# Pairing value loads by free cells, and the last output projection ahead of the last values, in a streaming attention decode kernel

## The chip, the cores and the metric

One core of a Trainium2 chip runs the whole kernel. The metric is the device time of one execution in microseconds (us), as the median of several. All executions quoted here are of the fast state; executions of one and the same kernel still spread by 0.4 to 1.5% (the changed kernel: 1161.5 to 1171.7 us in ten, 0.9%). Verdicts come from ratios: the mean time of one kernel's fast runs over that of the other's fast runs of the same rounds, with a 95% interval. Such a ratio is not quite the ratio of the medians that stand beside it.

## The reference, cut to what matters

Two layers, run twice over one batch of 8 with one query position each. D = 512, 32 query heads on 8 key/value heads, a cache of 8192 positions, head size 128, everything in bf16.

```python
x = A_x
x = x + attention(layernorm(x), A_k_cache, A_v_cache, A_wq, A_wo)
x = x + silu(layernorm(x) @ B_w1) @ B_w2
x = x + attention(layernorm(x), A_k_cache, A_v_cache, A_wq, A_wo)   # same caches, same weights
x = x + silu(layernorm(x) @ B_w1) @ B_w2
```

Keys of a batch are loaded once and used for both layers while they are on chip; values are loaded twice. That makes 465 MB from HBM for a few vectors of result.

## The kernel before: the parts that matter here

A small planner in the kernel lays out all work before the program is built: it simulates loads and engine work with assumed durations, gives each load a place in SBUF and decides the order of instructions on every engine. On the chip, loads are issued by one queue in that order, each as soon as the readers of its place are done. Values go through a ring of 7 cells of 4 KB per partition. One value head (2 MiB) is four quarters; a quarter is 128 rows of 4 KB, and two quarters side by side are one load of 8 KB rows. Before, the code says at each call whether a head comes as two halves or four quarters:

```python
RATE = {1: 2.57, 2: 2.51, 4: 2.48}     # assumed us per MiB for 1, 2, 4 cells
...
def load_v(b, g, q, cells):
    src = A_v_cache[b, g].rearrange("(p y) d -> p (y d)", p=128)
    return load_cells(f"v{b}.{g}.{q}", cells, [(lambda buf: buf, src[:, GR * q:GR * (q + cells)])])
...
# the calls
a_values(made[v], cells=1 if b >= 0 and i >= len(vs) - 3 else 2)
values(made[v], cells=1 if i < 2 else 2)
```

A load of two cells waits in the plan, and so in the queue's order, until two neighbouring cells are free.

The end of the program: wo (the weights of the output projection) for the last layer came in rows of 1 KB, behind three of the last six value heads:

```python
wo_v = A_wo.rearrange("(h p) d -> p h d", p=128)
...
for g, k in ((2, 0), (3, 1), (4, 2)):
    values(made[g], at=k)
load_wo_all()
for g, k in ((5, 5), (6, 6), (7, 7)):
    values(made[g], at=k)
# then: projection and feed-forward of batches 0..6, then those of batch 7
```

## Time and profile before

| | before |
|---|---|
| median of 3 runs | 1177.71 us (1177.63 to 1178.75) |
| span of the profiled run | 1177.4 us |
| DMA queue, share of 16 engines' span | 98.1% |
| busiest compute engine | PE, 61% |
| last value landing to the end | 15.3 us |

How to read it: the DMA share says that almost every us of the span is paid for by bytes in flight, so a us can be won in three ways only: bytes that move faster, engines that stop being idle, or a shorter piece after the last byte. The lines themselves stand in the prediction. In them PE is the matrix engine (PEld its weight loads), DVE, ACT and POOL are the engines for elementwise work, and an SPq line is the queue that issues loads.

### The profile page before, as it was taken

To read this page: it belongs to the slowest core of one execution; us is meant where nothing else is said; L and a number is where in the kernel's file an instruction comes from. 1 tells how busy PE (TensorE), PEld (TensorE's weight loads), DVE (VectorE), ACT (ScalarE), POOL (GpSimd) and SP (SyncE) were. 2 spreads that over 40 slices of the span, in tenths; PEclk is the share of its full clock that TensorE was granted. 3 is DMA by queue.
4 is the path that set the end of the run, shared out by engine and by line. 5 is a ranking of instruction groups with operands and counts; after the bars stand their busy time and mean duration, and the time that the engine had idled before them with its cause. 6 is when DMAs were issued, how large, how long until landed. Compare 5 with 4: busy or idle time off the path is not lost.

```text
span 1177.4 us, 32188 instructions
## 1 busy us (share of the span) xinstructions
PE 718.1 (61%) x13836; PEld 374.4 (32%) x13836; DVE 599.4 (51%) x1718; ACT 138.5 (12%) x477; POOL 117.5 (10%) x296
## 2 busy tenths in 40 slices
PE   2544556675565755666566665567556675565957
PEld 1222333242332423223232333224233242322535
DVE  5652356625565255733657245662556525573331
ACT  0010011111111111111111111111111111011110
POOL 1000011101111000100111001110111100010110
PEclk9655676757777577766667566775777666575775
DMA  9999799999999999999999999999999999999994
GB/s 365 421 420 338 307 421 420 413 403 400 415 407 411 387 413 417 414 404 386 422 423 413 401 404 410 410 404 395 409 416 403 408 394 408 419 415 394 400 394 167
DMA packets 85838, 467.15 MB, mean 397 GB/s; under 512 B 8880, under 2 KB 14784, under 8 KB 62144
## 3 DMA queue, kind: packets, MB, share of 16 engines
q1 hardware_dynamic: 85696, 465.10, 98.1%
q8 instruction: 109, 1.79, 0.6%
q14 instruction: 33, 0.27, 0.1%
HBM read 465.05 MB, written 0.01 MB: 395 GB/s over the span
## 4 chain that ended last, share of the span: by engine, by line
DMA 79%; PE 16%; issue 2%; DVE 1%; SPq 1%; ACT 0%; POOL 0%; POOLq 0%; DVEq 0%; ACTq 0%
DMA ring<-in_A_v_cache_dram 73%; PE ot L871 8%; PE sc L748 4%; DMA kts<-in_A_wo_dram 2%; DMA w<-in_B_w_dram 1%; DMA ring<-in_A_wq_dram 1%; PE misc L642 1%; PE yt L944 1%; DMA kts<-in_A_v_cache_dram 1%; PE sc L723 1%; SPq L340 0%; PE misc L510 0%; PE ex L893 0%; PE ex L915 0%; PE misc L492 0%
## 5 line engine op out<-in xcount | busy, mean ns | idle before, releaser
L871 PE MATMUL ot<-ring,p 128*8 128x256 bf16 x3904 | 243.5, 360 | 197.5 <-DMA ring<-in_A_v_cache_dram 195.8
L694 DVE STREAM_TRANSPOSE kts<-kts 128x1024 uint32<-128x1024 uint32 x256 | 309.1, 1226 | 36.8 <-DMA kts<-in_A_k_cache_dram 36.3
L748 PE MATMUL sc<-kts,bd 128*32 128x256 bf16 x4096 | 291.7, 406 | 34.4 <-DVE kts L694 24.8
L871 PEld LDWEIGHTS ot<-ring,p 128*8 128x8 bf16 x3904 | 73.5, 90 | 281.6 <-DMA ring<-in_A_v_cache_dram 261.2
L885 DVE TENSOR_TENSOR part<-ot,p 128x256 bf16<-128x256 f32 x128 | 54.2, 424 | 194.9 <-PE sc L748 95.1
L748 PEld LDWEIGHTS sc<-kts,bd 128*32 128x32 bf16 x4096 | 114.4, 117 | 103.2 <-DVE kts L694 34.1
L765 POOL PARTITION_ALL_REDUCE small<-small x128 | 47.8, 373 | 651.2 <-DVE small L761 536.6
L774 ACT ACTIVATE expd<-sc,small 128x256 bf16<-128x256 f32 x128 | 60.7, 475 | 416.1 <-DVE small L769 400.5
L881 ACT ACTIVATE p<-ot 128x256 bf16<-128x256 f32 x128 | 49.1, 384 | 469.5 <-PE ot L871 468.5
L780 PE MATMUL sc<-expd,ident 128*32 128x256 bf16 x512 | 42.8, 324 | 86.9 <-ACT expd L774 86.3
L794 POOL PARTITION_ALL_REDUCE small<-small x128 | 56.3, 440 | 197.7 <-DVE small L790 197.7
L760 DVE TENSOR_REDUCE small<-sc 128x1 f32<-128x256 f32 x128 | 53.3, 417 | 18.4 <-PE sc L748 18.4
L787 DVE STREAM_TRANSPOSE p<-sc 128x256 bf16<-128x256 bf16 x128 | 55.9, 437 | 9.3 <-PE sc L780 5.8
L731 DVE TENSOR_TENSOR bd<-sc,mask 128x64 bf16<-128x64 f32 x128 | 28.0, 219 | 56.2 <-PE sc L748 50.4
L780 PEld LDWEIGHTS sc<-expd,ident 128*32 128x32 bf16 x512 | 15.0, 107 | 126.2 <-ACT expd L774 126.0
L790 DVE TENSOR_SCALAR small<-hm,small 128x4 f32<-128x4 f32 x128 | 27.1, 212 | 37.1 <-ACT expd L774 37.1
L893 PE MATMUL ex<-diag,p 128*128 128x4 bf16 x256 | 25.5, 169 | 25.6 <-DVE part L885 23.2
L893 PEld LDWEIGHTS ex<-diag,p 128*128 128x128 bf16 x256 | 16.8, 103 | 73.5 <-ACT p L881 45.9
L944 PEld LDWEIGHTS yt<-z,ring 128*128 128x128 bf16 x1024 | 31.5, 101 | 26.1 <-issue 26.1
L944 PE MATMUL yt<-z,ring 128*128 128x4 bf16 x1024 | 36.4, 166 | 4.3 <-DVE z L922 4.0
L922 DVE TENSOR_TENSOR z<-ex,rc 128x16 bf16<-128x16 f32 x64 | 11.2, 174 | 54.6 <-PE ex L915 54.4
L723 PE MATMUL sc<-qab,sel 128*128 128x4 bf16 x256 | 16.3, 170 | 32.6 <-DVE rc L798 21.7
(84 smaller groups left out, 489.1 us busy)
## 6 DMA issues: line engine op xcount, KB each, us to landing
ring<-in_A_v_cache_dram SPq DMA_DIRECT2D x260, 512.0 KB, 8.2
kts<-in_A_k_cache_dram SPq DMA_DIRECT2D x64, 2048.0 KB, 11.2
ring<-in_A_v_cache_dram SPq DMA_DIRECT2D x114, 1024.0 KB, 11.7
ring<-in_A_wo_dram SPq DMA_DIRECT2D x64, 512.0 KB, 11.6
ring<-in_A_wq_dram SPq DMA_DIRECT2D x36, 512.0 KB, 9.6
kts<-in_A_v_cache_dram SPq DMA_DIRECT2D x5, 2048.0 KB, 16.7
kts<-in_A_wo_dram SPq DMA_DIRECT2D x2, 2048.0 KB, 27.0
w<-in_B_w_dram SPq DMA_DIRECT2D x2, 1792.0 KB, 14.7
```

The lines of the kernel that those rows point to most:

```text
L694: op(dve, lambda: dve.transpose(v, v), reads=[], writes=[res("kt", g)], add=(q > 0))
L748: steps.append(lambda t=t, y=y, w=w: pe.matmul(sc[32 * t:32 * t + 32, 0:256], w, kv[:, 2 * t + y, q], start=(q == 0 and y == 0), stop=(q = ...
L760: op(dve, lambda: dve.tensor_reduce(mxr[si], sv, AX.X, ALU.max), reads=[res(*scr)], writes=[res("mxr", si)])
L765: op(pool, lambda: pool.partition_all_reduce(mxa[si], mxp[si], 128, bass.bass_isa.ReduceOp.max), reads=[res("mxp", si)], writes=[res("mxa" ...
L774: op(act, lambda: act.activation(pe_out[:, :], sv, ACT.Exp, bias=bias[si], scale=SM_SCALE, accum_out=rsum[si]), reads=[res(*scr), res("bia ...
L780: steps = [lambda P=P: pe.matmul(sc[32 * P:32 * P + 32, 256:512], src[:, P], pe_out[:, :], start=True, stop=True) for P in range(4)]
L787: op(dve, lambda: dve.transpose(pt[:, :], src), reads=[res(*scr)], writes=[res("p", sm)])
L794: op(pool, lambda: pool.partition_all_reduce(ssa[si], ssm[si], 128, bass.bass_isa.ReduceOp.add), reads=[res("mxp", si)], writes=[res("mxa" ...
L871: steps.append(lambda t=t, c=c, k=k: pe.matmul(ot[32 * t:32 * t + 2 * R, 0:2 * DH], pt[:, k:k + 2 * R], vt[:, c, t], start=(P == 0 and c = ...
L881: op(act, lambda: act.activation(pt[:, :], ot[:, 0:2 * DH], ACT.Copy), reads=[res("ot", o)], writes=[res("p", sm)])
L885: op(dve, lambda: dve.tensor_tensor(part[:, :], ot[:, 0:2 * DH], pt[:, :], ALU.subtract), reads=[res("ot", o), res("p", sm)], writes=[res( ...
L944: steps.append(lambda j=j, dt=dt: pe.matmul(YT[:, dt * R:(dt + 1) * R], w[:, j, dt * 128:(dt + 1) * 128], zt[:, R * j:R * j + R], start=(g ...
```

## The change

Its intent: let the planner pair two quarters into a half wherever two cells side by side happen to be free, wait for a pair only while more than 2 us of transfers are still queued, and otherwise take a single cell; give wo of the last layer 4 KB rows; load it ahead of the last six value heads, so that the projection and feed-forward of batches 0 to 6 need not run at the very end. The core of the diff (cuts marked; the comments behind `#` in this and the later diffs are mostly added here, as labels):

```diff
-    RATE = {1: 2.57, 2: 2.51, 4: 2.48}
+    RATE = {1: 2.66, 2: 2.52, 4: 2.52}
+    ENOUGH = 2.0
...
+                        at = self.place(idle, n.cells)
+                        mate = n.mate if ... loads[li + 1] is n.mate and n.mate.left == 0 else None
+                        if mate:
+                            two = self.place(idle, 2)
+                            if two is not None:
+                                at = two
+                            else:
+                                mate = None
+                                if at is not None and wire - now > self.ENOUGH + 0.01:
+                                    at = None          # wait: enough is queued
...
-        values(h, cells=1)         # and the other calls
+        values(h)
...
-    wo_v = A_wo.rearrange("(h p) d -> p h d", p=128)
+    wo_v = A_wo.rearrange("(g p j) d -> p g (j d)", g=G, j=R)
...
-    for g, k in ((2, 0), (3, 1), (4, 2)):
-        values(made[g], at=k)
     load_wo_all()
...
+    for g, h in enumerate(made):
+        if g > 1:
+            values(h, at=g)
+        ...
+        w = out_proj_a(h, w, h["u"])      # per head, behind that head's values
```

With 4 KB rows four neighbouring rows of wo lie in one partition, so the attention output must be spread by a selection matrix and masked before the product (as layer 0 did already). The selection matrices become stride-4 views of four identities.

More of the change, by code (lines that the diff above doesn't have):

```diff
@@ L115 @@
 class Node:
-    __slots__ = ("eng", "dur", "emit", "prio", "deps", "outs", "left", "ready", "end", "take", "give", "name", "cells")
+    __slots__ = ("eng", "dur", "emit", "prio", "deps", "outs", "left", "ready", "end", "take", "give", "name", "cells",
+                 "mate", "span")
     def __init__(self, name, eng, dur, emit, prio, deps):
@@ L133, in __init__ @@
         self.cells = 0
+        self.mate = None
+        self.span = 1
 class Plan:
-    RATE = {1: 2.57, 2: 2.51, 4: 2.48}
+    RATE = {1: 2.66, 2: 2.52, 4: 2.52}
+    ENOUGH = 2.0
     LAND = 5.0
@@ L188, in run @@
         wire = 0.0
+        alarm = 0.0
         idle = set(cells)
@@ L200, in run @@
                     n = loads[li]
-                    at = self.place(idle, n.cells) if n.take else None
+                    at = mate = None
+                    if n.left == 0 and n.take:
+                        at = self.place(idle, n.cells)
+                        mate = n.mate if li + 1 < len(loads) and loads[li + 1] is n.mate and n.mate.left == 0 else None
+                        if mate:
[6 more added lines that the diff above has]
+                                    at = None
+                                    if wire - self.ENOUGH > alarm:
+                                        alarm = wire - self.ENOUGH
+                                        heapq.heappush(events, (alarm, seq, "alarm", n))
+                                        seq += 1
                     if n.left == 0 and (at is not None or not n.take):
@@ L205, in run @@
                             idle -= set(range(at, at + n.cells))
+                        dur = n.dur
+                        if mate:
+                            n.span = 2
+                            mate.give = at + 1
+                            mate.span = 0
+                            idle.discard(at + 1)
+                            dur = self.RATE[2]
                         order.append((now, seq, n))
                         seq += 1
-                        wire = max(wire, now + 0.1) + n.dur
+                        wire = max(wire, now + 0.1) + dur
                         heapq.heappush(events, (wire + self.LAND, seq, "done", n))
@@ L211, in run @@
                         li += 1
+                        if mate:
+                            order.append((now, seq, mate))
+                            seq += 1
+                            heapq.heappush(events, (wire + self.LAND, seq, "done", mate))
+                            seq += 1
+                            li += 1
                         moved = True
@@ L277, in _build @@
     w2_sb = sb([128, FT, D], BF16, "w2")
-    ident = sb([128, 128], BF16, "ident")
+    ident4 = sb([128, 4 * 128], BF16, "ident")
+    ident = ident4[:, 0:128]
     cst = sb([128, 5], BF16, "cst")
-    sel = sb([128, 4, 4, 32], BF16, "sel")
     mask = sb([128, 4], BF16, "mask")
@@ L315, in _build, with rows_of @@
     EX = bank("ex")
+    def rows_of(j):
+        return ident4[:, :].rearrange("p (k j) -> p j k", j=4)[:, j]
     syn = Sync(nc, ctx)
@@ L381, in load_cells, with load_v, emit @@
         return n
-    def load_v(b, g, q, cells):
+    def load_v(b, g, q, before=None):
         src = A_v_cache[b, g].rearrange("(p y) d -> p (y d)", p=128)
-        return load_cells(f"v{b}.{g}.{q}", cells, [(lambda buf: buf, src[:, GR * q:GR * (q + cells)])])
+        n = plan.load(f"v{b}.{g}.{q}", 1, None)
+        def emit():
+            if n.span:
+                dma(sp, gran(n.give, n.span), src[:, GR * q:GR * (q + n.span)], rsem[n.give],
+                    writes=[res("ring", n.give + k) for k in range(n.span)])
+        n.emit = emit
+        if before is not None:
+            before.mate = n
+        return n
     def load_k(b, g):
@@ L397, in load_wo @@
     def load_wo(g):
-        return load_cells(f"wo{g}", 1, [
-            (lambda buf: buf, A_wo.rearrange("(g p j) d -> g p (j d)", g=G, j=R)[g])])
+        return load_cells(f"wo{g}", 1, [(lambda buf: buf, wo_v[:, g])])
     def frees(n, src):
@@ L407, in _build @@
     big_hs = tail[:, 512:512 + FT * NB]
+    big_y = tail[:, 768:768 + 2 * NB * KT].bitcast(FP32)
     def norm_nodes(tag, prio, b0, nb, deps):
@@ L543, in consts @@
             fill=0.0, base=0, channel_multiplier=1), writes=[res("ident")])
-        iv = ident[:, :].rearrange("p (j k) -> p k j", k=4)
-        for a in range(4):
-            op(pool, lambda a=a: pool.tensor_copy(sel[:, :, a, :], iv), reads=[res("ident")], writes=[res("sel")])
+        for a in range(1, 4):
+            op(pool, lambda a=a: pool.tensor_copy(ident4[:, 128 * a:128 * (a + 1)], ident[:, :]),
+               reads=[res("ident")], writes=[res("ident")])
         op(pool, lambda: pool.memset(mask[:, :], 0.0), writes=[res("mask")])
@@ L701, in keys @@
         count[0] += 1
+        own_rows = layer == 0 or b == NB - 1
         pr = FIRST + 4 if first else u
@@ L723, in expand @@
                 steps.append(lambda fe=fe: pe.matmul(
-                    qx[:, R * fe:R * fe + R], sel[:, fe].rearrange("p a j -> p (a j)"), qsrc, start=True, stop=True))
-            mms(steps, reads=[res("sel"), qres], writes=[res(*scr)])
+                    qx[:, R * fe:R * fe + R], rows_of(fe), qsrc, start=True, stop=True))
+            mms(steps, reads=[res("ident"), qres], writes=[res(*scr)])
         def spread():
@@ L798, in rec @@
             op(dve, lambda: dve.reciprocal(rcp[sm], ssa[si]), reads=[res("mxa", si)], writes=[res("rcp", sm)])
-            if layer == 0:
+            if own_rows:
                 op(dve, lambda: dve.tensor_tensor(rcm[sm], rcp[sm], mask[:, :], ALU.mult),
@@ L814, in keys @@
         sc_users.append((sn, n4))
-        return dict(layer=layer, b=b, g=g, u=u, sm=sm, exp=n4, rc=n7)
+        return dict(own_rows=own_rows, b=b, g=g, u=u, sm=sm, exp=n4, rc=n7)
     ot_users = []
     es = []
+    z_users = {}
     def load_v_slot(b, g, k):
@@ L837, in load_v_slot, with values @@
         return got
-    def values(h, wo=None, cells=2, at=None):
-        layer, b, g, u, sm = h["layer"], h["b"], h["g"], h["u"], h["sm"]
+    def values(h, wo=None, wo_at=2, at=None):
+        b, g, u, sm = h["b"], h["g"], h["u"], h["sm"]
         pr = count[0] - 1 if b < NB - 1 else u + 1
@@ L849, in values @@
         vs = []
+        loads = []
         for P in range(4):
-            if P == (2 if cells == 2 else 3) and wo is not None:
+            if P == wo_at and wo is not None:
                 h["wo"] = load_wo(wo)
@@ L854, in values @@
                 vn = quarters[P][0]
-            elif P % cells == 0:
-                vn = load_v(b, g, P, cells)
+            else:
+                vn = load_v(b, g, P, loads[-1] if loads else None)
+                loads.append(vn)
             def pv(P=P, vn=vn):
@@ L864, in pv @@
                 else:
-                    vt, held_in = gran(vn.give, cells)[:, GR * (P % cells):GR * (P % cells + 1)], cells_of(vn)
+                    vt, held_in = gran(vn.give), cells_of(vn)
                 vt = vt.rearrange("p (c t n) -> p c t n", c=2, t=4)
@@ L875, in values @@
             n = plan.add(f"v{u}.{P}", "PE", 0.4, pv, pr, [h["exp"], vn, old or clear_n] + vs[-1:])
-            if not quarters and P % cells == cells - 1:
+            if not quarters:
                 frees(n, vn)
@@ L900, in values @@
         es.append(plan.add(f"g{u}", "PE", 0.2, gather, pr - 2, [ln, back(ot_users, 1)]))
-        if layer == 1:
+        if not h["own_rows"]:
             def norm():
@@ L915, in spread @@
                 steps = [lambda j=j: pe.matmul(
-                    EX[:, 8 + R * j:8 + R * j + R], sel[:, j].rearrange("p a k -> p (a k)"), attna[:, hd],
+                    EX[:, 8 + R * j:8 + R * j + R], rows_of(j), attna[:, hd],
                     start=True, stop=True) for j in range(R)]
-                mms(steps, reads=[res("sel"), res("attna", g)], writes=[res("ex")])
+                mms(steps, reads=[res("ident"), res("attna", g)], writes=[res("ex")])
             def own():
@@ L928, in values @@
             n = plan.add(f"spread{u}", "PE", 0.2, spread, pr - 2, [n])
-            h["n"] = plan.add(f"own{u}", "DVE", 0.17, own, pr - 2, [n, h["rc"]])
+            h["n"] = plan.add(f"own{u}", "DVE", 0.17, own, pr - 2, [n, h["rc"], z_users.get(o)])
             h["z"] = o
@@ L932, in values, with out_proj_a @@
         p_users[sm] = [vs[-1], h["n"]]
-    def out_proj_a(h, prev):
+    def out_proj_a(h, prev, prio):
         g, wn, o = h["g"], h["wo"], h["z"]
@@ L939, in mul @@
         def mul():
-            w = gran(wn.give).rearrange("p (j d) -> p j d", j=R)
+            w, held_in = h["wo_in"]()
+            w = w.rearrange("p (j d) -> p j d", j=R)
             steps = []
@@ L947, in mul @@
                         skip_group_check=True))
-            mms(steps, reads=cells_of(wn) + [res("z", o)], writes=[res("yt")], add=g > 0)
-        n = plan.add(f"w{h['u']}", "PE", 0.56, mul, count[0] - 3, [h["n"], wn, prev])
-        frees(n, wn)
-        return n
-    def out_proj_b(tag, g, b0, nb, deps):
+            mms(steps, reads=held_in + [res("z", o)], writes=[res("yt")], add=g > 0)
+        n = plan.add(f"w{h['u']}", "PE", 0.56, mul, prio, [h["n"], wn, prev])
+        z_users[o] = n
+        return n
@@ new lines, in out_proj_b, with spread, own @@
+    def out_proj_b(tag, g, nb, prev, deps):
+        prio = count[0] + 20
+        hd = slice(R * g, R * g + R)
+        n_c = nb * R
+        zb = tail[:, 1024 + R * n_c * (g % 2):1024 + R * n_c * (g % 2 + 1)]
+        def spread():
+            steps = [lambda j=j: pe.matmul(
+                EX[:, 32 + n_c * j:32 + n_c * (j + 1)], rows_of(j), qab[:, 0:nb, hd], start=True, stop=True)
+                for j in range(R)]
+            mms(steps, reads=[res("ident")] + [res("attnb", g, b) for b in range(nb)], writes=[res("ex")])
+        def own():
+            op(dve, lambda: dve.tensor_tensor(
+                zb.rearrange("p (n h) -> p n h", h=R),
+                EX[:, 32:32 + R * n_c].rearrange("p (n h) -> p n h", h=R),
+                mask[:, :].unsqueeze(1).to_broadcast([128, R * nb, R]), ALU.mult),
+                reads=[res("ex"), res("mask")], writes=[res("ring", 1)])
@@ L956, in mul @@
         def mul():
-            w = slot(WO_AT[g // 4]).rearrange("p (h d) -> p h d", h=16)
+            w = slot(WO_AT[g // 4]).rearrange("p (g j d) -> p g j d", g=4, j=R)[:, g % 4]
             steps = []
-            for r in range(R):
+            for j in range(R):
                 for dt in range(KT):
-                    steps.append(lambda r=r, dt=dt: pe.matmul(
-                        YT[:, dt * nb:(dt + 1) * nb], w[:, R * (g % 4) + r, dt * 128:(dt + 1) * 128],
-                        qab[:, b0:b0 + nb, R * g + r],
-                        start=(g == 0 and r == 0 and dt == 0), stop=(g == G - 1 and r == R - 1),
+                    steps.append(lambda j=j, dt=dt: pe.matmul(
+                        YT[:, dt * n_c:(dt + 1) * n_c], w[:, j, dt * 128:(dt + 1) * 128],
+                        zb[:, n_c * j:n_c * (j + 1)],
+                        start=(g == 0 and j == 0 and dt == 0), stop=(g == G - 1 and j == R - 1),
@@ L965, in mul @@
                         skip_group_check=True))
-            mms(steps, reads=[res("wo_all", g // 4)] + [res("attnb", g, b) for b in range(b0, b0 + nb)],
-                writes=[res("yt")], add=g > 0)
-        return plan.add(f"{tag}.w{g}", "PE", 0.56, mul, count[0] + (20 if nb > 1 else 0), deps)
+            mms(steps, reads=[res("wo_all", g // 4), res("ring", 1)], writes=[res("yt")], add=g > 0)
+        n = plan.add(f"{tag}.sp{g}", "PE", 0.2, spread, prio, deps + zb_own[-1:])
+        zb_own.append(plan.add(f"{tag}.own{g}", "DVE", 0.25, own, prio, [n] + zb_mul[-2:-1]))
@@ L971, in _build, with a_values @@
+        zb_mul.append(plan.add(f"{tag}.w{g}", "PE", 0.56, mul, prio, [zb_own[-1], wo_all[g // 4], prev]))
+        return zb_mul[-1]
+    zb_own = []
+    zb_mul = []
     free_yt = [None]
     y_now = [None]
-    def a_values(h, cells=2):
-        values(h, wo=h["g"], cells=cells)
-        y_now[0] = out_proj_a(h, y_now[0] if h["g"] else free_yt[0])
+    def a_values(h, wo_at=2):
+        values(h, wo=h["g"], wo_at=wo_at)
+        wn = h["wo"]
+        h["wo_in"] = lambda: (gran(wn.give), cells_of(wn))
+        y_now[0] = out_proj_a(h, y_now[0] if h["g"] else free_yt[0], count[0] - 3)
+        frees(y_now[0], wn)
@@ L984, in load_ffn, with x2_node @@
             sp, w2_sb[:, :, :], B_w2.rearrange("(ft p) d -> p ft d", p=128), wsem["w2"], writes=[res("w2")]), ring=False))
-    def x2_node(b, prio):
+    def x2_node(tag, b0, nb, prio, deps):
+        ys = ysum[:, :] if nb == 1 else big_y[:, 0:KT * nb]
         def add():
             op(dve, lambda: dve.tensor_reduce(
-                ysum[:, :], YT[:, 0:KT * R].rearrange("p (k h) -> p k h", h=R), AX.X, ALU.add),
-                reads=[res("yt")], writes=[res("ysum")])
-            op(dve, lambda: dve.tensor_tensor(xs[:, b, :], ysum[:, :], xs[:, b, :], ALU.add),
+                ys, YT[:, 0:KT * nb * R].rearrange("p (k h) -> p k h", h=R), AX.X, ALU.add),
+                reads=[res("yt")], writes=[res("ysum")] + ([] if nb == 1 else [res("ring", 1)]))
+            op(dve, lambda: dve.tensor_tensor(
+                xs[:, b0:b0 + nb, :], ys.rearrange("p (k b) -> p b k", b=nb), xs[:, b0:b0 + nb, :], ALU.add),
                reads=[res("ysum"), res("xs")], writes=[res("xs")])
-        return plan.add(f"c{b}.x2", "DVE", 0.3, add, prio, [y_now[0]])
-    WO_AT = (3, 4)
+        return plan.add(f"{tag}.x2", "DVE", 0.3, add, prio, deps)
+    WO_AT = (0, 1)
     wo_all = []
@@ L1002, in emit @@
             def emit(i=i, k=k):
-                dma(sp, slot(k).rearrange("p (h d) -> p h d", h=16), wo_v[:, 16 * i:16 * i + 16, :], ksem[k],
+                dma(sp, slot(k).rearrange("p (g n) -> p g n", g=4), wo_v[:, 4 * i:4 * i + 4, :], ksem[k],
                     writes=[res("kt", k), res("wo_all", i)])
@@ L1030, in _build @@
         if b >= 0:
-            n = x2_node(b, prio)
+            n = x2_node(f"c{b}", b, 1, prio, [y_now[0]])
             free_yt[0] = n
@@ L1064, in _build @@
             if v[0] == 0:
-                a_values(made[v], cells=1 if b >= 0 and i >= len(vs) - 3 else 2)
+                a_values(made[v])
             else:
-                values(made[v], cells=1 if i < 2 else 2)
+                values(made[v])
                 ends.append(made[v])
@@ L1071, in _build @@
             load_ffn()
-    def x2_of(tag, b0, nb, prio, deps):
-        def add():
-            op(dve, lambda: dve.tensor_tensor(
-                xs[:, b0:b0 + nb, :], YT[:, 0:KT * nb].rearrange("p (k b) -> p b k", b=nb), xs[:, b0:b0 + nb, :],
-                ALU.add), reads=[res("yt"), res("xs")], writes=[res("xs")])
-        return plan.add(f"{tag}.x2", "DVE", 0.2, add, prio, deps)
     fin = NB - 1
@@ L1083, in _build @@
     made = [keys(1, fin, g, second_q[g], first=g == 0, buf=g % (N_P + N_DEF)) for g in range(G - 1)]
-    values(made[0], cells=1)
+    values(made[0])
     made.append(keys(1, fin, G - 1, second_q[G - 1], buf=0))
-    values(made[1], cells=1)
-    for g, k in ((2, 0), (3, 1), (4, 2)):
-        values(made[g], at=k)
+    values(made[1])
     load_wo_all()
-    for g, k in ((5, 5), (6, 6), (7, 7)):
-        values(made[g], at=k)
     w = free_yt[0]
@@ L1094, in _build @@
     for g in range(G):
-        w = out_proj_b("d", g, 0, fin, [w, wo_all[g // 4]] + done)
-    n = x2_of("d", 0, fin, count[0] + 20, [w])
-    fed = ffn_nodes("d", count[0] + 20, 0, fin, [n, second_q[G - 1]])
-    w = n
-    for g in range(G):
-        w = out_proj_b("e", g, fin, 1, [made[g]["n"], w])
+        w = out_proj_b("d", g, fin, w, done)
+    w = x2_node("d", 0, fin, count[0] + 20, [w])
+    fed = ffn_nodes("d", count[0] + 20, 0, fin, [w, second_q[G - 1]])
+    for g, h in enumerate(made):
+        if g > 1:
+            values(h, at=g)
+        h["wo"] = wo_all[g // 4]
+        h["wo_in"] = lambda g=g: (
+            slot(WO_AT[g // 4])[:, GR * (g % 4):GR * (g % 4 + 1)], [res("wo_all", g // 4)])
+        w = out_proj_a(h, w, h["u"])
     big = count[0] + 10
-    n = x2_of("e", fin, 1, big, [w])
+    n = x2_node("e", fin, 1, big, [w])
     n = ffn_nodes("e", big, fin, 1, [n, fed])
```

## The prediction

> **What bounds the kernel now.** I read the page first (busy shares, the slices, the chain that ended last), then the DMA part, then stretches of the span by window, then the PE timeline of the end.
>
> ```profile
> PE 718.1 (61%) x13836; PEld 374.4 (32%) x13836; DVE 599.4 (51%) x1718; ACT 138.5 (12%) x477; POOL 117.5 (10%) x296
> DMA  9999799999999999999999999999999999999994
> GB/s 365 421 420 338 307 421 420 413 403 400 415 407 411 387 413 417 414 404 386 422 423 413 401 404 410 410 404 395 409 416 403 408 394 408 419 415 394 400 394 167
> DMA 79%; PE 16%; issue 2%; DVE 1%; SPq 1%; ACT 0%; POOL 0%; POOLq 0%; DVEq 0%; ACTq 0%
> q1 hardware_dynamic: 85696, 465.10, 98.1%
> ```
>
> No compute engine passes 61%; the DMA row is 9 in every slice but slice 5 and the last. The hardware queue's packets fill 98.1% of 16 engines' span and the chain is 79% DMA. So the kernel is a stream of 465 MB, and its time is bytes over rate, plus one hole, plus a tail. The second row of the waits (PE on the value tiles, 195.8 us) is the compute side waiting for that stream, not a cost of its own. Rate differs by slice (386 to 423 GB/s), and that is what the change is after.
>
> The windows tell the rates of the different loads apart (columns: stretch, length, engines, clock, DMA share, GB/s):
>
> ```profile
> core 0: us, PE busy (x) PEld busy (x) DVE busy (x) ACT busy (x) POOL busy (x), PEclk, DMA share, GB/s
> 512.00:542.00 30.00, 21.23 (x468) 11.62 (x464) 6.71 (x29) 3.22 (x12) 1.96 (x4) 0.56 1.03 409
> 566.00:632.00 66.00, 40.15 (x752) 20.77 (x744) 42.32 (x117) 8.43 (x30) 7.64 (x19) 0.72 1.01 420
> 544.00:561.00 17.00, 8.56 (x160) 3.50 (x152) 9.59 (x26) 1.92 (x7) 1.63 (x4) 0.70 0.99 377
> 119.00:129.50 10.50, 6.63 (x174) 5.06 (x174) 1.66 (x8) 0.39 (x2) 0.56 (x1) 0.50 0.48 187
> ```
>
> The first is a run of value quarters (512 KB, rows of 4 KB): 409 GB/s, 2.56 us per MiB. The second is keys in 16 KB rows with value halves in 8 KB rows: 420 GB/s, 2.50 us per MiB. The third is the start of a pass, where quarters follow the first key tile: 377 GB/s with the engines still full. The fourth is the one real hole, where the second layer's first keys wait for the first feed-forward.
>
> The end:
>
> ```profile
> 1130.55 1.05 PE L871 MATMUL ot<-kts,p 128*8 128x256 bf16 x32 [0.48 <-DMA kts<-in_A_v_cache_dram]
> 1135.56 1.88 PE L871 MATMUL ot<-kts,p 128*8 128x256 bf16 x32 [1.55 <-DMA kts<-in_A_v_cache_dram]
> ...
> 1141.52 1.87 PE L961 MATMUL yt<-qab,kts 128*128 128x7 bf16 x64 [2.74 <-DMA kts<-in_A_wo_dram]
> 1147.41 1.87 PE L961 MATMUL yt<-qab,kts 128*128 128x7 bf16 x64 [4.02 <-DMA kts<-in_A_wo_dram]
> ...
> 1156.99 1.60 PE L492 MATMUL misc<-xn,w 128*128 128x7 bf16 x54
> 1159.75 0.21 PE L492 MATMUL misc<-xn,w 128*128 128x7 bf16 x2 [1.16 <-issue]
> ...
> 1161.63 1.66 PE L510 MATMUL misc<-ring,w 128*128 128x7 bf16 x56
> 1163.21 2.73 PE L871 MATMUL ot<-kts,p 128*8 128x256 bf16 x48
> 1165.87 0.21 PE L893 MATMUL ex<-diag,p 128*128 128x4 bf16 x2
> ```
>
> Work that starts on a landing dates it: 2 MiB of values in 16 KB rows take 1135.56 - 1130.55 = 5.0 us, 2 MiB of wo in 1 KB rows 1147.41 - 1141.52 = 5.9 us. After that PE does the seven batches' output projection and feed-forward (L961 x7, L492, L510) while the last values land, and takes up the last six value steps only at 1163.21. The last landing's semaphore stands in the trace at 1162.1, so 15.3 us of the 1177.4 come after the stream.
>
> **What the Trainium skill says.** "DMA: Bandwidth & Descriptors", section "Why small descriptors are slow (HBM only)", gives a fixed cost per packet inside the DMA engine and fixed descriptor bytes per operation, and counts merging as worthwhile mainly at 256 B and less. The trace agrees on the sign and shows a penalty at larger sizes: grouped by size, the packets of the trace last 51 ns at 1 KB, 166.6 at 4 KB, 315.4 at 8 KB, 629.7 at 16 KB, which is 20.1, 24.6, 26.0 and 26.0 GB/s per engine. So 4 to 8 KB is worth something, 8 to 16 nothing. "Perfetto Trace Analysis", section "DMA Optimizations", says that going from 2 KB to 4 or 8 KB can help dramatically; here the step from 4 to 8 is at most 5%. "HBM Reference", "Specifications (TRN2)", says that a lone core reads at about 425 GB/s; the best slice here is 423, so halves are already at the ceiling. "TensorE: Matmul & The Clock Gate", "Weight-path perf modes", says that fast weight load takes strided weights; this matters for the selection matrices, which become stride-4 views. The trace agrees as far as it goes: the swap at L780 reads 32 columns of the identity at that stride in 107 ns, the contiguous 128 columns at L723 take 103.
>
> **The change part by part.** I counted the loads of both built programs.
>
> Part 1, pairs. Before: 114 value halves and 260 quarters through the ring. After: 136 halves and 216 quarters. Bytes are equal; 44 quarters become 22 halves, 22 MiB out of 444. That is small because most places already had halves: the first pass even loses 3 (16 to 13), and the seven passes in the middle and the last gain 25. Of these 25, 14 sit right behind the first key tile of a pass (the 377 GB/s place), 11 elsewhere.
> - The 11: by windows 2.56 - 2.50 = 0.06 us per MiB, by packets (166.6 ns a quarter row, 315.4 a half row) 0.14. I take 0.09: 1.0 us.
> - The 14: in the packets of the trace the four quarters there cost 5.5 to 5.9 us per 2 MiB in each of the seven passes, 40.2 in all; as halves at the usual 2.51 per MiB they would cost 35.1. That is 5.0 us if the slowness goes with the row length. It may instead belong to the moment (the queue had nearly drained just before), so I take 60%: 3.0 us.
> - The first pass: its last halves ran at 2.8 to 3.2 us per MiB because they were issued only 1 to 2.3 us ahead of their data; quarters can go as soon as one cell is free. I take 0.5 us.
> Sum 4.5 us, with 1 to 7 as reasonable.
>
> Part 2, wo of the last layer in 4 KB rows: 4 MiB at 5.9 us per 2 MiB becomes 2.56 per MiB, so 11.8 - 10.2 = 1.6 us off the stream.
>
> Part 3, wo ahead of the last values. The bytes are the same, so the stream ends no sooner for it, but the seven batches' projection and feed-forward can now run behind 12 MiB of values, 30 us of transfer, instead of among the last 3. In the built program's PE order they stand before the last 128 value matmuls (four heads); the last projection is per head, behind each head's values. The new tail, from the last landing, with durations of the profile: one value step 0.6; copy, subtract and gather 1.3 (as from 1165.9 to 1167.2 now); the new cast, spread and own-row multiply 0.2 + 0.35 + 0.25 (L911 174 ns, L915 0.25 us, L922 174 ns, with hops); projection 0.6; two adds 0.5 in place of one; from there 9.2 to the end (1168.2 to 1177.4, unchanged feed-forward, transpose, store). Sum 13.0, and 0.2 for the head before it still on PE: 13.2 against 15.3, so 2.1 us.
>
> Part 4, the selection matrices as strided views, one pool copy less, 8 more mask multiplies of 165 ns, 32 spread matmuls: off the path, 0.
>
> Total 4.5 + 1.6 + 2.1 = 8.2 us: 1177.7 - 8.2 = 1169.5.
>
> **Rivals.** (a) Waiting for pairs drains the queue. A half needs two neighbours, so its load goes later than a quarter's would; in the first pass of the trace late-issued halves ran at 2.8 to 3.2 us per MiB. Against it: a load of 8 KB rows issued 2.5 to 3.5 us ahead of its data still ran at 2.52 here (5 cases), quarters so issued at 2.70, and issue only waits for the assigned cells' own readers, not for the planner's clock. If it held for a quarter of the halves, it would eat some 6 us: about 1176. (b) The slow place behind the first key tile is of the moment, not of the row length; then part 1 is worth 1.5 us and the time is about 1172.5. (c) The slow place vanishes with all that hangs on it: the window lost 17 x (1 - 377/420) = 1.7 us in this pass, about 12 over seven; then about 1162. (d) The end gains nothing, because PE still runs late behind the moved work; for it speaks that PE runs at half clock there, against it that PE is busy a third of the time between the landings of wo: 1171.5. (e) The hole at 119 to 129.5 stays in any case, for nothing in its chain changes.
>
> **Range and chances.** The three parts can each miss by about their own size and are partly independent: 1162 to 1177. A gain over 2% needs 1154 or less, more than all I can find even with (c) and the full tail; a loss over 2% would need a new hole of 24 us in a stream that is 98% full. Faster 2%, same 97%, slower 1%.
>
> **What would show it.** Right: the DMA queue again near 98% full; quarters' windows still about 409 and the stretch behind each pass's first key tile above 400 GB/s; the two wo landings about 5.1 us apart and ahead of the values; the last value landing near 1156 and about 13 us behind it. Wrong: slices of the DMA row at 8 or less in the middle passes, or longer stalls of the load queue on value matmuls with low GB/s (rival a); 377 GB/s unchanged at the pass starts (b); L541 or L559, the feed-forward of seven batches, still between the last landings and the last value steps (d).

## The result, and the profile after

1163.93 us median (four runs, 1162.26 to 1169.97) against 1177.67 (four runs); ratio 0.9897, interval 0.9857 to 0.9938. In the first experiment, with five rounds: 1163.16 against 1177.29, ratio 0.9886 (0.986 to 0.9913). So 13 to 14 us were won where 8.2 were predicted; the time lies in the predicted range, near its lower end, and within 2%.

The page of the changed kernel: busy shares, the DMA rows of the slices, the queue and the chain that ended last.

```profile
PE 723.6 (62%) x13900; PEld 390.6 (34%) x13900; DVE 603.1 (52%) x1736; ACT 139.9 (12%) x485; POOL 116.8 (10%) x295
DMA  9999799999999999999999999999999999999993
GB/s 370 420 421 400 324 418 424 412 401 417 421 418 411 413 418 421 416 394 415 416 419 414 407 415 419 416 409 402 423 407 408 394 406 421 420 408 382 400 423 160
q1 hardware_dynamic: 79456, 465.09, 98.3%
DMA 72%; PE 21%; issue 4%; DVE 2%; POOL 1%; SPq 1%; ACT 0%; POOLq 0%; DVEq 0%; ACTq 0%
```

The queue is as full as before (98.3%) with the same bytes in fewer packets (79456 for 85696): by the page's own share, the gain is rate and not removed idleness. The first large difference in the GB/s row is the fourth slice, 338 before and 400 now.

To see where the time came from I took, from the DMA records of each trace, the end of the last packet of certain loads, and cut the span there. Several experiments below share the same stream of loads in the same order up to the last pass, so one program has several profiles; that shows the spread. Passes are the stretches in which one batch's keys are loaded; seven of them follow the first.

| stretch, us | before | old pairs, other end | changed stream, five profiles | mean of these |
|---|---|---|---|---|
| start to first feed-forward weight | 114.9 | 113.5 | 109.6, 109.8, 110.4, 110.0, 111.0 | 110.2 |
| from there to the first key tile of pass 2 | 22.0 | 21.9 | 21.7, 21.8, 22.0, 21.6, 21.9 | 21.8 |
| first to second key tile, seven passes in all | 75.9 | 77.2 | 70.7, 70.6, 70.0, 70.9, 69.7 | 70.4 |
| rest of the seven passes | 849.4 | 850.0 | 845.7, 843.5, 846.0, 843.6, 849.7 | 845.7 |
| last key tile to last value packet | 99.5 | 98.4 | 97.3, 98.4, 97.4, 99.5, 99.3 | 98.4 |

("Old pairs, other end" is the tail-alone experiment; the five profiles are the changed kernel twice and three experiments that touch only its end.) The hole behind the first feed-forward is unchanged, as predicted. The first pass gives some 3 to 5 us, the pass starts 5 to 7, the rest of the passes about 4, where one program alone spreads by 6, and the end of the stream about 1.

The first pass, in the same window of both kernels (stretch, length, engines, clock, DMA share, GB/s), and what the load queue did. Before:

```profile
88.00:106.00 18.00, 8.86 (x153) 4.48 (x154) 7.48 (x19) 1.68 (x6) 0.80 (x2) 0.50 0.89 328
```

```profile
84.02 7.30 SPq L340 DMA_DIRECT2D ring<-in_A_v_cache_dram  x2
91.38 0.42 SPq L340 DMA_DIRECT2D ring<-in_A_wo_dram  x1
95.14 3.13 SPq L340 DMA_DIRECT2D ring<-in_A_v_cache_dram  x2
99.36 0.33 SPq L340 DMA_DIRECT2D ring<-in_A_wo_dram  x1
102.72 0.33 SPq L340 DMA_DIRECT2D ring<-in_A_v_cache_dram  x1
103.10 0.98 SPq L340 DMA_DIRECT2D w<-in_B_w_dram  x2
```

After:

```profile
88.00:106.00 18.00, 10.44 (x184) 4.88 (x184) 6.87 (x16) 1.68 (x6) 0.80 (x2) 0.60 1.03 410
```

```profile
86.00 0.80 SPq L379 DMA_DIRECT2D ring<-in_A_v_cache_dram  x2
89.72 0.33 SPq L379 DMA_DIRECT2D ring<-in_A_wo_dram  x1
90.10 5.42 SPq L379 DMA_DIRECT2D ring<-in_A_v_cache_dram  x4
96.13 1.01 SPq L379 DMA_DIRECT2D ring<-in_A_wo_dram  x1
97.25 1.44 SPq L379 DMA_DIRECT2D ring<-in_A_v_cache_dram  x2
98.74 0.98 SPq L379 DMA_DIRECT2D w<-in_B_w_dram  x2
```

Before, the last value halves of the first pass are issued with gaps of 3 to 5 us, and the engines move 328 GB/s at a DMA share of 0.89. What the queue waited for between 84 and 106 us (us in total, times, longest):

```profile
SPq L91 <- PE ot L871: 13.9, 4, 6.6
```

That is PE still reading the values in the cells to be filled; a half needs two such cells side by side. Afterwards quarters follow one another and the same window moves 410. The feed-forward weights are issued 4.4 us sooner. In 18 us the difference is worth 18 x (1 - 328/410) = 3.6 us, an estimate from the two rates. This gain comes from *fewer* pairs.

The start of the fourth middle pass, the window that ran at 377 GB/s before, now 11.5 us earlier:

```profile
532.50:549.50 17.00, 8.23 (x152) 3.81 (x144) 9.66 (x26) 1.97 (x7) 1.62 (x4) 0.70 1.03 420
```

420 GB/s: the slow place is gone in this run. The window that lies the same way to the first key tile moved 420, 412, 408 and 394 GB/s in the four other profiles of the changed stream, so one window alone proves little; the table's sum over seven passes is the better measure.

The end (PE timeline of the changed kernel):

```profile
1127.98 1.66 PE L541 MATMUL misc<-xn,w 128*128 128x7 bf16 x56
1129.57 0.60 PE L924 MATMUL ot<-kts,p 128*8 128x256 bf16 x8
1130.35 1.66 PE L559 MATMUL misc<-ring,w 128*128 128x7 bf16 x56 [0.18 <-DVE ring L551]
...
1133.47 0.19 PE L946 MATMUL ex<-diag,part 128*128 128x4 bf16 x2 [1.42 <-issue]
...
1137.53 0.19 PE L946 MATMUL ex<-diag,p 128*128 128x4 bf16 x2 [1.09 <-DVE part L938]
...
1143.23 2.73 PE L924 MATMUL ot<-kts,p 128*8 128x256 bf16 x48
...
1147.75 0.39 PE L924 MATMUL ot<-kts,p 128*8 128x256 bf16 x8
```

The last landing's semaphore stands at 1145.29 in this trace, but the last value step (L924 x8) starts at 1147.75, 2.46 us later. PE was still at the heads before it: the seven batches' feed-forward (L541, L559) and an issue gap of 1.4 us put it 3 us behind the landings, and in program order each head then waits about 1.1 us for its subtraction before the gather. From the last landing to the end: 15.2 us, as before (15.3). That part of the gain did not come.

### The profile page after: what moved, and what is told of

It reads as the page before. It is cut to its first block, busy times and chain, and to the rows that moved or that the text cites. A ratio compares the mean times of both kernels' runs of the same rounds, so it can differ in the third digit from the quotient of the medians.

```text
span 1160.5 us, 32290 instructions
## 1 busy us (share of the span) xinstructions
PE 723.6 (62%) x13900; PEld 390.6 (34%) x13900; DVE 603.1 (52%) x1736; ACT 139.9 (12%) x485; POOL 116.8 (10%) x295
## 3 DMA queue, kind: packets, MB, share of 16 engines
q1 hardware_dynamic: 79456, 465.09, 98.3%
q8 instruction: 109, 1.79, 0.6%
## 4 chain that ended last, share of the span: by engine, by line
DMA 72%; PE 21%; issue 4%; DVE 2%; POOL 1%; SPq 1%; ACT 0%; POOLq 0%; DVEq 0%; ACTq 0%
DMA ring<-in_A_v_cache_dram 66%; PE ot L924 9%; PE sc L798 5%; DMA kts<-in_A_v_cache_dram 2%; DMA w<-in_B_w_dram 1%; PE misc L691 1%; PE misc L559 1%; DMA ring<-in_A_wq_dram 1%; PE misc L541 1%; PE yt L998 1%; DMA kts<-in_A_k_cache_dram 1%; POOL rstd L506 1%; PE ex L946 1%; DVE part L938 0%; PE sc L773 0%
## 5 line engine op out<-in xcount | busy, mean ns | idle before, releaser
L924 PE MATMUL ot<-ring,p 128*8 128x256 bf16 x3904 | 239.3, 359 | 168.6 <-DMA ring<-in_A_v_cache_dram 165.2
L924 PEld LDWEIGHTS ot<-ring,p 128*8 128x8 bf16 x3904 | 78.5, 93 | 247.9 <-DMA ring<-in_A_v_cache_dram 220.5
L938 DVE TENSOR_TENSOR part<-ot,p 128x256 bf16<-128x256 f32 x128 | 54.2, 424 | 200.1 <-PE sc L798 97.3
L819 DVE SCALAR_TENSOR_TENSOR small<-small,hm 128x4 f32<-128x4 f32 x128 | 18.8, 147 | 28.3 <-POOL small L815 27.9
## 6 DMA issues: line engine op xcount, KB each, us to landing
kts<-in_A_k_cache_dram SPq DMA_DIRECT2D x64, 2048.0 KB, 11.5
w<-in_B_w_dram SPq DMA_DIRECT2D x2, 1792.0 KB, 13.7
```

Source lines behind the costliest of these rows:

```text
L924: steps.append(lambda t=t, c=c, k=k: pe.matmul(ot[32 * t:32 * t + 2 * R, 0:2 * DH], pt[:, k:k + 2 * R], vt[:, c, t], start=(P == 0 and c = ...
L938: op(dve, lambda: dve.tensor_tensor(part[:, :], ot[:, 0:2 * DH], pt[:, :], ALU.subtract), reads=[res("ot", o), res("p", sm)], writes=[res( ...
```

## The experiments

Theory 1 is the sum of the prediction: pairs 4.5 us, wo rows 1.6, the end 2.1. Its rivals are that the end is worth most, that pairs drain the queue, and that the slow places are of the moment and not of the row length. Twelve kernels ran; the first four on one chip, the others on another, each beside the kernel before. "The end" below is the time from the semaphore of the last value landing to the end of the span.

**The changed kernel again.** No edit.

> The changed kernel itself, for its spread on this chip. Theory 1 (the sum of the prediction, sizes off by luck): near 1169, ratio 0.993. Theory 2 (the first four runs, 1162 to 1170, are typical): 1163 to 1165, ratio 0.988 to 0.990, last value landing some 14 us sooner than before, and about 13 us from there to the end.

1163.16 us (1161.53 to 1171.74), ratio 0.9886. Theory 1's size is out, the first result stands. Its last landing to the end: 15.4 us.

**The end alone.** The changed kernel with the old fixed pairs and the old assumed rates.

```diff
-                vn = load_v(b, g, P, loads[-1] if loads else None)
+            elif P % cells == 0:
+                vn = load_vc(b, g, P, cells)      # as before: 114 halves, 260 quarters
```

> The new end (wo in 4 KB rows ahead of the last values, projection per head) with the old fixed pairs, 114 halves and 260 quarters. The prediction's sum gives 1.6 for the rows and 2.1 for the end: 3.7 us, so 1174. Rival 1, the end is worth most of the gain: 1166 or less. Rival 2, the end is worth nothing since PE lags behind: 1177.

1176.32 us, ratio 0.9987 (0.9953 to 1.0021). The rival that the end is worth most falls. The predicted 3.7 us would make a ratio of 0.997, which the interval does not exclude; the trace says more. Its stream between last keys and last values is 1.1 us shorter than before (98.4 for 99.5), from the wo rows; its end is 15.7 us.

**The pairs alone.** The kernel before with the new planner rule and loads, old end.

```diff
-        values(h, cells=1)
+        values(h)                  # and all other calls, with the new planner
```

> The new pairing (136 halves, 216 quarters) with the old end. The prediction's sum gives 4.5 us: 1173. If the pairs are what was under-estimated, 8 to 10 us: 1168 to 1170. If pairs only drain the queue: 1178 or more. With the end alone it should add up to the whole change within 2 us, unless the parts work on each other.

1166.83 us, ratio 0.990 (0.9875 to 0.9924): 1.0% of the change's 1.1%. The two parts add up (0.990 and 0.9987 make 0.9887 against 0.9886), and the pairs (with the new assumed rates, which this edit carries too) were what had been under-estimated.

**No pairs at all.**

```diff
-            before.mate = n
+            pass
```

> The changed kernel with every value quarter loaded alone (488 quarters, no half). 136 MiB go from 8 KB rows to 4 KB rows. By packets, 0.14 us per MiB, that costs 19 us; by windows, 0.06 us per MiB, 8 us: so 1172 to 1183 if row length is what counts. If instead quarters keep the queue fuller (a load goes as soon as one cell is free), part of it comes back and the time is under 1170.

1176.88 us, ratio 0.9987 (0.9962 to 1.0012). 136 halves are worth 1176.88 - 1163.16 = 13.7 us, or 0.10 us per MiB, between the windows' 0.06 and the packets' 0.14. This is a net figure: it holds what halves win by their rows and what they lose by going later. And with the same new end, this kernel without one half is as fast as the end-alone kernel with its 114 fixed ones (1176.32, the same ratio of 0.9987). In the first pass it has the short time of the changed kernel (110.7 us to the first weight, 114.9 before), in the rest of the passes it takes longer (853.6 for 849.4). So 114 fixed halves were worth nothing against none. In the first pass the traces show that they lost by waiting; that they lost the rest in the same way is inferred.

**Halves in the first pass again**, 16 instead of 11 ahead of the feed-forward weights, the rest by the new rule (139 halves in all for 136).

```diff
-                                if at is not None and wire - now > self.ENOUGH + 0.01:
+                                if n.must:              # value loads of the first pass
+                                    at = None
+                                elif at is not None and wire - now > self.ENOUGH + 0.01:
```

> The changed kernel, but in the first pass every value load is a half again (16 instead of 11 before the feed-forward weights), as in the kernel before; all later passes keep the new rule. Theory A, the first pass lost about 5 us to loads that waited for two neighbouring cells: 1168, and the first feed-forward weight lands about 4 to 5 us later than in the changed kernel. Theory B, the prediction's 0.5 us: 1164.

1164.74 us, ratio 0.9877 (0.9846 to 0.9909). The times don't show the loss: it is inside their spread. Its trace does:

```profile
88.00:106.00 18.00, 9.26 (x168) 4.81 (x168) 6.79 (x16) 1.68 (x6) 0.80 (x2) 0.60 0.96 355
```

355 GB/s where the changed kernel has 410; the first weight lands at 112.4 us, against 109.6 to 111.0 in five profiles. The other traces settle what the times cannot. All five kernels with 16 halves there (before, end alone, rates alone, only pairs, this one) move 327 to 355 GB/s in this window and land the first weight at 112.4 to 114.9 us; all nine with 11 or none move 398 to 410 and land it at 109.6 to 111.0. Under the new planner, this kernel and the one with only pairs (113.5 us) put the cost of forced halves at about 2 to 3 us; the rest of the 3 to 5 us between the kernels belongs to something else of the new plan.

**Quarters at the pass starts**, behind the first key tile in seven passes.

```diff
-            before.mate = n
+            if not (g == 1 and 0 <= late_b == b):     # second layer, seven passes
+                before.mate = n
```

> The changed kernel, but the eight quarters... four value quarters behind the first key tile of each of seven passes stay single (14 halves fewer nearby, 118 halves in all). If row length makes that place slow: its 4 to 5 us come back, 1168, and the stretch from the first to the second key landing grows from about 10.1 to 10.8 us per pass. If the place is slow for other reasons: 1164 to 1165.

1173.98 us, ratio 0.9947 (0.9903 to 0.9991), against the changed kernel's 0.9886 (0.986 to 0.9913): the intervals just touch, so it is probably slower, by some 0.6%, and above both expected times. The seven pass starts take 73.6 us, 3.2 more than the changed stream's 70.4 and still 2.3 less than before. The same window in its trace:

```profile
542.00:559.00 17.00, 8.91 (x160) 4.08 (x152) 9.65 (x26) 2.02 (x7) 1.63 (x4) 0.70 1.01 391
```

391 GB/s, between 377 and 420. About 3 us of the pass starts' 5 come back with the short rows. The other 2 are no larger than what plans with quarters in that place differ by: 73.0 (no pairs), 73.6 (this one), 73.9 (rates alone, below), 75.9 (before) and 77.2 (end alone), against 69.6 to 71.2 in the eight traces with halves there, the kernel with only pairs, below, among them. So which of it is the moment is not shown. The rest of its loss (851.4 us in the rest of the passes) goes with four further halves lost elsewhere (118 instead of 122), with a different plan and with spread; that is not taken apart.

**Only pairs.** No quarter is ever taken alone.

```diff
-    ENOUGH = 2.0
+    ENOUGH = -1e9
```

> The changed kernel with no value quarter ever loaded alone: 244 halves, each load waiting for two neighbouring cells however long. By row length alone, 108 MiB from 4 to 8 KB rows at 0.06 to 0.14 us per MiB, it would gain 6 to 15 us on the changed kernel: 1149 to 1157. If waiting drains the queue (the prediction's first rival), it is slower than the changed kernel: 1175 or more, with a lower DMA share and loads issued under 2.5 us ahead of their data.

1207.86 us, ratio 1.024 (1.0209 to 1.0271): slower than the kernel before. The DMA rows of its page:

```profile
DMA  9999799999999999999999999999999999999994
GB/s 368 421 419 362 317 419 422 378 328 414 421 419 385 368 422 422 413 351 387 417 415 386 363 400 419 423 367 349 422 403 408 356 374 421 420 419 349 345 411 175
```

The fastest slices stay at 419 to 423, but two in each of the seven passes fall to 328 to 387, where heads follow one another without keys between: from the last key tile of one pass to the first of the next, six times over, it takes 339.7 us, 304.8 in the changed kernel, and from the last key tile of all to the last value 106.5 for 97.3. That is 44 of the 47 us between the two profiles. A tenth of its value, key and weight loads in rows of 4 KB and more is issued less than 1.6 us ahead of the first packet (2.8 in the changed kernel), as halves wait until two neighbours are free. The DMA row shows nine tenths all the same. The prediction's first rival is true of a kernel that goes this far. With the rule that gives up a pair once no more than 2 us are queued it does not show; no other threshold was tried.

**The assumed rates alone**, in the kernel before.

```diff
-    RATE = {1: 2.57, 2: 2.51, 4: 2.48}
+    RATE = {1: 2.66, 2: 2.52, 4: 2.52}
```

> The kernel before with nothing but the planner's three assumed rates changed to the new ones; the loads stay 114 halves and 260 quarters in the same order, only the places of instructions and cells can shift. If the new assumed rates do part of the work: under 1174. If they do nothing: 1177, ratio 0.997 to 1.003.

1185.79 us, ratio 1.0048 (1.0012 to 1.0084): a little slower. In the old planner the new rates win nothing; under the new rule they were not tried apart. The list of loads is the same as before in every size and order, so a change of the plan that moves no load to another row length can shift the time by half a per cent, some 6 us. Differences of that size above and below (quarters at the pass starts, the rest of the passes) can be the plan and not the row length.

**The end without the seven batches' feed-forward** (a wrong result on purpose).

```diff
-    fed = ffn_nodes("d", count[0] + 20, 0, fin, [w, second_q[G - 1]])
+    fed = w
```

> The changed kernel without the seven batches' norm and feed-forward at the end (a wrong result on purpose). In the changed kernel the last value step starts 2.4 us after its landing, behind head work that ran late since that feed-forward, and the end is 15.2 us as before. If that lag is why the new end saved nothing: the last landing to the end takes 13.0 to 13.3 us here, as the prediction's sum has it. If the lag comes from the heads' own chain on PE: still 15 us.

13.4 us from the last landing to the end, for 15.2: the lag theory holds. Its PE timeline at the last heads:

```profile
1141.26 1.88 PE L924 MATMUL ot<-kts,p 128*8 128x256 bf16 x32 [0.24 <-DMA kts<-in_A_v_cache_dram]
1143.73 1.02 PE L924 MATMUL ot<-kts,p 128*8 128x256 bf16 x16 [0.59 <-DMA kts<-in_A_v_cache_dram]
...
1146.59 0.60 PE L924 MATMUL ot<-kts,p 128*8 128x256 bf16 x8
```

Now the value steps wait for their landings, and the last starts 0.4 us behind its own (1146.16). One trace of each kernel is enough here: in the seven traces with the new end as it is (the changed kernel twice, and five experiments) the end takes 14.9 to 15.7 us, in three with the old one 15.3 to 15.5. (The run as a whole is no faster by its median, 1164.6 with ratio 0.9879, 0.9836 to 0.9922: 2 us drown in the spread of four runs.)

**wo behind three of the last six value heads**, 4 KB rows kept.

```diff
+    early = {g: load_v_slot(fin, g, g) for g in (2, 3, 4)}
     load_wo_all()
```

> The changed kernel with wo of the last layer (still in 4 KB rows) behind the third of the last six value loads, where the kernel before has it. The stream moves the same bytes. If loading wo ahead matters only by what PE still has to do at the end: the last landing to the end grows to 16.5 to 19 us, 1165 to 1167. If it does not matter: 15.2 us and 1163.

17.2 us from the last landing to the end, 1165.32 us, ratio 0.9892 (0.9851 to 0.9933). In its timeline the seven batches' products stand between the last value steps:

```profile
1146.47 1.65 PE L541 MATMUL misc<-xn,w 128*128 128x7 bf16 x56
...
1150.49 1.65 PE L559 MATMUL misc<-ring,w 128*128 128x7 bf16 x56
...
1152.52 0.29 PE L968 MATMUL ex<-attna,ident 128*128 128x4 bf16 x4 [0.27 <-ACT attna L964]
```

So with the new projection, loading wo ahead is worth 2 us of the end (17.2 to 15.2); and with wo late, the new form of the projection ends 1.9 us later than the old one did (17.2 for 15.3). By these traces the two cancel.

**An attempt to beat both: one feed-forward for all eight batches.** The norm of seven batches stays early; up and down run once, at the end, on 8 columns.

```diff
-    fed = ffn_nodes("d", count[0] + 20, 0, fin, [w, second_q[G - 1]])
+    fed = norm_nodes("d.ln", count[0] + 20, 0, fin, [w, second_q[G - 1]])
...
-    n = ffn_nodes("e", big, fin, 1, [n, fed])
+    n = norm_nodes("e.ln", big, fin, 1, [n, fed])
+    n = ffn_nodes("e", big, 0, NB, [n], norm=False)
```

> An attempt to beat both: the norm of the seven batches stays early, but their up and down products are done at the end with the last batch's, 8 columns in the same 112 matmuls. It takes 3.3 us of PE work from in front of the last heads. If the lag theory holds: the end is 13.0 to 13.6 us, the time 1161 to 1162. If not: 15.2 and 1163.

The end takes 14.0 us, 1.2 less, less than hoped since the wider products wait longer for the elementwise steps (1.79 us for the normalized input, 1.42 in the changed kernel). The time is 1167.13 us, with runs from 1158.73 to 1175.72; ratio 0.9896 (0.985 to 0.9943). Its load list is the changed kernel's and its edit touches only the end, yet in its profile the last value landed 6 to 8 us later than in the changed stream's four other profiles; why is open. It holds the shortest run of the study and is not shown to be faster.

**The same, with three value quarters ahead of the key tile that waits** behind the first feed-forward.

```diff
+    by = {n.name: n for n in plan.loads}
+    plan.loads.remove(by["k1.0"])
+    plan.loads.insert(plan.loads.index(by["v0.1.2"]) + 1, by["k1.0"])
```

> The same, and in the hole behind the first feed-forward three value quarters are loaded ahead of the first key tile of the second pass, which waits for its cell there. They fill 3.9 us of some 5 us in which nothing is loaded: 1157 to 1158 if the bytes moved forward are all gained, 1161 to 1162 if the hole only moves or the three lost pairs and a new plan take it back.

1164.76 us, ratio 0.9875 (0.9842 to 0.9908): not told apart from the changed kernel. In the window 115 to 131 us it moves 335 GB/s where the changed kernel moves 242, so much of the hole was filled; and the end takes 13.6 us. But four pairs were lost, and the rest of the passes took 850.1 us for 845.7. What is won in the hole is not seen in the time: neither 1157 to 1158 nor 1161 to 1162 was reached, and which part takes it back is not shown.

## Why the prediction was right, and which of its terms were not

**Bound.** Right: a stream at 98% of the queue, before and after, and a gain that comes from its rate.

**The first pass, 0.5 us predicted.** Mis-sized. It measured 3.3 to 4.7 us in the traces (114.9 and 113.5 down to 110.2), with 328 GB/s against 410 in the window; about 2 of them come back when the halves are forced again. The prediction had read the late issue and the slow packets there, but priced only the packets' durations and not the gaps between them. The sign stood in its own lines: slice 4 of the GB/s row has 338 at a DMA row of 9, which the reading "386 to 423 GB/s" leaves out. This is the largest miss whose cause is shown.

**The pass starts, 3.0 us predicted** as 60% of 5.0. Mis-sized. Measured 5.5 for seven passes (75.9 down to 70.4); 3.2 of these come back when quarters are put back (73.6). That this is the predicted 3.0 is as near as can be said, since plans with quarters there spread from 73.0 to 77.2; where the other 2 come from is open.

**The other pairs, 1.0 us predicted.** 0.10 us per MiB, as the kernel without pairs shows, makes 1.1 for 11 MiB. The rest of the passes gained about 4 us in the mean, more than these pairs account for; five profiles of one program spread by 6 us there, and the pairs alone had 849.7, so the surplus is not settled. One sign failed here unremarked: quarters' windows were to stay at about 409 GB/s, and the window 500 to 530 us moves 391 to 396 in four profiles of the changed stream.

**wo in 4 KB rows, 1.6 us predicted.** About right: the end of the stream takes 97.3 to 99.5 us with the new rows in six profiles, mean 98.4, and 99.5 to 100.7 in three with the old.

**wo ahead of the last values, 2.1 us predicted.** Wrong; it gave nothing (15.2 and 15.4 us for 15.3). The step that failed is "the new tail, from the last landing": each duration in it was right, and without the seven batches' feed-forward the end indeed takes 13.4 us for the predicted 13.2. But it started from a free PE. The prediction's rival (d), PE still behind the moved work, is what happened, though not in the form of its sign: the feed-forward itself (L541, L559) ends at 1132.0, 13 us ahead of the last landing, and it is the heads behind it that run late. In the changed kernel's trace the fifth to seventh heads' values land at 1130.4, 1135.3 and 1140.3, and PE takes them up 3.2, 2.4 and 2.9 us later, so the lag of the feed-forward is not paid back by the last landing. The signs named about 1156 us for the last landing and 13 us from there to the end; it was 1145.3 and 15.2.

**The strided views, 0 predicted.** The times cannot show a cost this small, and the support was weak: it set 32 strided columns (L780) beside 128 contiguous ones (L723). In the changed kernel's trace a load of 128 strided columns (L773) lasts 118 ns by its median, where L723 took 104 and 99 before; no run tries this alone.

**The rivals.** (a) shown to be real in the kernel with pairs only, and not seen with the rule. (b) not settled: row length counts there, and how much of the rest is the moment stays open. (c) at the starts yes, without the 12 us; its sum is also off, since 12 us in place of the 3.0 make 1160.5 and not 1162. (d) true. (e) true.

**The sum.** 8.2 predicted, 13 to 14 measured: too little for the first pass, the starts and perhaps the rest of the passes, too much for the end. That the time fell into a range of 15 us is in part luck: errors of both signs were added, and the range was wide. A slip in the readings: from 24.6 to 26.0 GB/s is nearly 6%, not "at most 5%".

## What to carry to other kernels

A longer row is worth its rate only if the load is not issued later for it: here 114 fixed pairs were worth nothing against none, all pairs cost 2.4%, and pairs taken when free, and given up once only 2 us of work were still queued, were worth about 1%. A DMA row at nine tenths did not mean full rate here (328 to 387 GB/s in slices of the kernel with only pairs); compare GB/s by window, and look at the gaps between issues where it dips. Work moved off the end helps only if the engine that runs it has caught up by the time the last data lands: look at how long after its landing the last step starts.

## What the Trainium skill lacked or had wrong

- "DMA: Bandwidth & Descriptors", section "Why small descriptors are slow (HBM only)": its remark that packetization is only worth it at 256 B and less is about joining consecutive descriptors into packets. It has no figure for longer rows at these sizes: here rows of 4 KB joined to 8 KB were worth 13.7 us in 1177 for 136 MiB, 0.10 us per MiB, and nothing is gained from 8 to 16 KB (26.0 GB/s per engine by the packets in both).
- "Perfetto Trace Analysis", section "DMA Optimizations", advises larger transfers, and names splitting, which lets some start sooner, for DMA engines that are generally idle. Here splitting paid with the queue 98% full. With a ring of few cells the larger transfer waits for its place: loads of 8 KB rows only took 1207.9 us, 2.4% more than the kernel before, at 328 to 387 GB/s in the slices concerned.
- No page found says how far ahead of its data a load must be issued for full rate. In the first pass before, halves issued 1 to 2.3 us ahead of their first packet ran at 2.8 to 3.2 us per MiB by their packets, and halves issued 2.7 us ahead or more at 2.5 (one at 2.7).
